# Keeping Softplus's table loaded, converting one weight group a tile, and letting the second MLP begin after one chunk

## The chip, the cores and the metric

The kernel runs on one core of one Trainium2 chip. The metric is the device time of one execution in microseconds (us), a median of several runs. PE is TensorE, DVE is VectorE, ACT is ScalarE, POOL is GpSimd; SP issues the DMAs.

## What is computed

Top-32 attention over 4 batches of 8 heads (576 rows, head size 64), then two MLPs on its 2304 x 512 output, the first with a softplus between its two matrices, the second with h - tanh(h). The weights arrive as float64.

```python
scores = scale * np.matmul(q, k.transpose(0, 1, 3, 2))
kth = np.partition(scores, -32, axis=-1)[..., -32:-31]
scores = np.where(scores >= kth, scores, -1e9)
attn = np.exp(scores - scores.max(-1, keepdims=True))
attn = attn / (attn.sum(-1, keepdims=True) + 1e-09)
x = np.matmul(attn, v)              # then heads side by side: 2304 x 512
h = x @ w_in;  x = (np.maximum(h, 0) + np.log1p(np.exp(-np.abs(h)))) @ w_out
h = x @ w2_in; out = (h - np.tanh(h)) @ w2_out      # 512 -> 2048 -> 512, both
```

## The kernel before

**Attention** goes in 144 tiles of 128 query rows (one head and one batch each; 16 of them gather the rows that are left over). A tile runs through a pipeline: `front` (L582) makes the 128 x 576 scores on PE and ACT copies them out (L585, tile `ssb`); `chain` finds the 32nd largest on DVE with four MAX8 (L594) and three MATCH_REPLACE8 (L597), so that four MAX8 are one tile in every count below; `exps` takes the exponential on ACT; `turn` splits it into two 16-bit halves (L624 on ACT, L625 and L626 on POOL) and a DMA transposes them (L628, issued by SP); `back` multiplies by v (L640 to L645).

`exps` has two forms. With the table set of the exponential loaded, it is two ACT instructions over 128 x 576 (L134, out `ssb` and then out `x`). With Softplus's set loaded it is one (L134, out `x`); `mask` then adds a multiplication on DVE (L618) and a scaling on ACT (L619). Which form a tile takes follows from the set that is loaded as the program is written down. `set_table` (L128) loads a set.

**Weights** come in 32 groups, 8 for each of the four matrices, converted from float64 to two 16-bit halves by `conv_step`: two DVE passes (L316, L334), three ACT passes (L306, L310, L335), POOL (L342, L346), eight small PE matmuls (L192) and a DVE reduction (L199). A pass is over 128 x 1024, or four times over 128 x 256 where a group is loaded in quarters into spare x buffers. Groups 0 to 15 are the first MLP's, 16 to 31 the second's. `WPS` = 2 groups are issued a tile for the first 16 and `WPS2` = 0.5 after that, from tile 8 on; groups after the sixteenth get a lower priority than the attention.

**The MLPs** go in ten chunks: two of 256 rows for each batch, and two of 128 rows for the rows left over (each after two batches). A chunk is 8 steps of the first MLP and 8 of the second; a step (`mlp_step`) is `gemm1` (24 matmuls, L708 to L710), `act1` (Softplus or Tanh at L134, L727 on DVE for the second MLP, L729 on ACT, L730 and L733 on POOL) and, some steps later, `gemm2` (24 matmuls of 256 columns at L751 to L753 in the first MLP, 12 of 512 columns at L759 to L761 in the second). `y_finish` turns the first MLP's result into the second's input. A chunk can begin when its last attention tile is through, at tiles 19, 39, 55, 75 and so on.

**The planner**: each tile hands out one step of 256 rows (or two of 128). `next_step` picks: the second MLP of a chunk that waits when all 32 groups are converted, at least `MINC` chunks have begun, and two chunks wait (`AHEAD`); else the first MLP of the next chunk that is ready; else, with the same conditions on groups and `MINC`, the second MLP of a waiting chunk; else nothing, and the tile's step is lost (only one is carried over). A scheduler then places the instructions on each engine by priority; the engines run them in that fixed order.

Of the kernel before, what the change touches and what calls it, by code (L numbers as in the profile page):

```python
# [18 lines left out]
EXP_SET = "exp_and_others"  # L19
# [16 lines left out]
KE = 'P'  # L36
NQH = 1
OWN = 3
MINC = 2
HPW = 100  # L40
HPW2 = 0
MKN = 0
# [31 lines left out]
def topk_attention_two_mlps(  # L74
# [29 lines left out]
    NG = NF // 2  # L104
# [17 lines left out]
    def set_table(name):  # L122
        if table[2] == name:
            return
        with ExitStack() as es_:
            for i in table[1] or [table[0]]:
                es_.enter_context(tc.issue_after(i.ins))
            table[0] = nc.scalar.preload_act_table_set(name)  # L128
        table[1], table[2] = [], name
# [673 lines left out]
    def run_gemm2(stp):  # L803
        ch = stp.ch
        if stp.g == 0:
            acc = new_acc(ch.T)
            if stp.m == 0:
                ch.acc1 = acc
            else:
                ch.acc2 = acc  # L810
        stp.acc = ch.acc1 if stp.m == 0 else ch.acc2
        gemm2(stp)
        if stp.g == NG - 1:
            if stp.m == 0:
                y_finish(ch)
            else:
                out_finish(ch)
# [4 lines left out]
    def mlp_step(ch, m, g):  # L822

        if m == 1 and g == 0:
            while any(s.ch is ch and s.m == 0 for s in pend):
                run_gemm2(pend.pop(0))
        stp = Step()
        stp.ch, stp.m, stp.g, stp.T = ch, m, g, ch.T
        if m == 0:
            if g == 0:  # L830
                set_table(SP_SET)
                key = f"l{ch.b // 2}" if ch.left else f"b{ch.b}"
                if key not in scales1:
                    scales1[key] = chunk_scales(ch.ix if ch.left else ix[ch.b], 0, 1.0, "a" + key)
                ch.sc1 = scales1[key]
                ch.ic1 = ch.sc1[2]
            stp.x = ch.x
            stp.sc = ch.sc1
        else:
            if g == 0:  # L840
                set_table(EXP_SET)
                if not hasattr(ch, "sc2"):
                    ch.sc2 = second_scales(ch.sy, ch.iy)
            stp.x = ch.y
            stp.sc = ch.sc2
        gemm1(stp)
        if g == NG - 1 and m == 1:
            xy_free.extend(stp.x.slots)
        with tc.high_priority(100):
            act1(stp)  # L850
        if g == NG - 1 and m == 0:
            set_table(EXP_SET)
        pend.append(stp)
        while len(pend) > (LAG if ch.T == 2 * P else LAG1):
            run_gemm2(pend.pop(0))
# [81 lines left out]

    wloaded, wconv = [], []
    WPS = 2
    WPS2 = .5  # L940
    wi, wcred = [0], [0.0]
    wq = [(i, g) for i in range(4) for g in range(NG)]

# [35 lines left out]
    def next_step(n):  # L979

        if phase[0] is None:
            can1 = c1[0] < len(order) and order[c1[0]][1] <= n
            can2 = wdone[0] == 4 * NG and c1[0] >= MINC
            if can2 and len(kept) >= AHEAD:
# [23 lines left out]
    def emit_steps(n, budget):  # L1008
        nonlocal_credit[0] += budget
        while nonlocal_credit[0] > 0:  # L1010
            st = next_step(n)
            if st is None:
                nonlocal_credit[0] = min(nonlocal_credit[0], 1.0)
                return
            mlp_step(*st)
            nonlocal_credit[0] -= st[0].T / 256.0
# [24 lines left out]
    for n in range(-1, NT + 2 + BL):  # L1041
# [36 lines left out]
        if n >= 0:  # L1078
# [3 lines left out]
            if n in v_norm_at and n > 0:  # L1082
                b = v_norm_at[n]
                v_norm(b)
                if b % 2:
                    nc.vector.tensor_tensor(sxl[b // 2], sx[b - 1], sx[b], op=ALU.min)
                    nc.vector.tensor_tensor(ixl[b // 2], ix[b - 1], ix[b], op=ALU.max)
                    for c in (b - 1, b):
                        nc.vector.tensor_mul(fl[c], sxl[b // 2], ix[c])
            wcred[0] += WPS if wi[0] < 16 else (WPS2 if n >= W2N else 0)  # L1090
            while wcred[0] >= 1:
# [12 lines left out]
    while (st := next_step(NT)) is not None:  # L1104
        mlp_step(*st)
# [32 lines left out]
```

## Time and profile before

| | us |
|---|---|
| median of 3 runs | 1326.21 (1322.19 to 1329.95) |
| the profiled execution | 1331.09 |
| its span, first to last instruction | 1329.4 |
| PE busy (81%) | 1071.8 |
| DVE busy (75%) | 992.9 |
| ACT busy (70%) | 935.0 |
| POOL busy (63%) | 833.9 |

How to read the profile: a busy time is the time in which an engine had an instruction running; matmuls are pipelined, so a busy PE isn't one at its peak. The line of slices cuts the span into 40 equal parts, a digit for the busy tenths of each. PEclk, or the granted clock, is the share of TensorE's full clock. A row of windows gives for a stretch of time the busy time of each engine with, in brackets, the number of its instructions.

### The profile page before, as it was taken

Reading aid. Unit: us, or ns where it says so; the run is one execution under the profiler, and the core shown is the slowest. Engines: PE = TensorE matmul, PEld = TensorE weight load, DVE = VectorE, ACT = ScalarE, POOL = GpSimd, SP = SyncE. Lnnn points to the kernel's source line nnn. Section 1 sums busy time; section 2 is a strip of 40 time slices with the busy share of each in tenths; the row PEclk is TensorE's granted clock in tenths of the full one; section 3 lists DMA queues with packets and bytes.
Section 4 is the critical chain, followed back from the end, with each engine's and each line's share of the span. In section 5 each row is a group of like instructions: output and inputs, shape, how many; then the busy total and the mean of one; then the engine's idle time right before and its main releaser. Section 6 shows DMA issues by size and latency. Waiting matters only on the chain.

```text
span 1329.4 us, 28005 instructions
## 1 busy us (share of the span) xinstructions
PE 1071.8 (81%) x9992; PEld 834.9 (63%) x9992; DVE 992.9 (75%) x2208; ACT 935.0 (70%) x1824; POOL 833.9 (63%) x1196
## 2 busy tenths in 40 slices
PE   3242436894358998999899999999999799999998
PEld 2241325673236866767677886686767677886975
DVE  5997988989889498986899699849978699620011
ACT  7967868787777688775877777668866777743332
POOL 3879776676766666664678566657855466543332
PEclk9999998895558899998899999999999899999999
DMA  9956787357647647553455344545654345200000
GB/s 283 302 141 192 211 224 174 82 122 159 149 116 172 137 97 156 132 97 91 92 126 140 72 92 86 96 90 100 139 85 94 72 92 95 41 14 9 9 9 17
DMA packets 322524, 153.17 MB, mean 115 GB/s; under 512 B 270160, under 2 KB 302416, under 8 KB 322384
## 3 DMA queue, kind: packets, MB, share of 16 engines
q1 hardware_dynamic: 322384, 151.39, 49.5%
q8 instruction: 78, 1.28, 0.4%
q14 instruction: 62, 0.51, 0.1%
HBM read 73.04 MB, written 15.37 MB: 67 GB/s over the span
## 4 chain that ended last, share of the span: by engine, by line
PE 37%; DMA 14%; DVE 13%; ACT 13%; POOL 12%; issue 8%; SPq 2%; POOLq 0%; ACTq 0%; DVEq 0%
PE h L710 5%; PE h L708 5%; PE h L709 5%; DMA pT<-hl 5%; DVE m L594 4%; DVE x L597 4%; POOL hl L625 3%; PE y L760 2%; PE y L759 2%; PE y L761 2%; PE y L751 2%; PE y L752 2%; PE y L753 2%; PE s L582 2%; POOL g L733 2%
## 5 line engine op out<-in xcount | busy, mean ns | idle before, releaser
L594 DVE MAX8 m<-x 128x8 f32<-128x576 f32 x432 | 318.1, 748 | 2.7
L625 POOL TENSOR_TENSOR hl<-x,hl 128x512 f16<-128x512 f32 x144 | 173.1, 1202 | 96.2 <-ACT hl L624 86.8
L730 POOL TENSOR_SCALAR r<-r,gs 128x512 f32<-128x512 f32 (+1 forms) x160 | 110.5, 691 | 177.0 <-ACT g L729 164.1
L597 DVE MATCH_REPLACE8 x<-m,x 128x576 f32<-128x576 f32 x288 | 213.1, 740 | 0.0
L733 POOL TENSOR_TENSOR g<-r,g 128x512 f16<-128x512 f32 (+1 forms) x160 | 173.2, 1084 | 9.1
L708 PE MATMUL h<-y,whi 128*128 128x256 f16 (+1 forms) x640 | 164.4, 266 | 9.7 <-ACT y L779 9.3
L708 PE MATMUL h<-x,whi 128*128 128x256 f16 (+1 forms) x640 | 165.6, 268 | 4.1 <-DMA x<-xs 3.6
L751 PE MATMUL y<-g,whi 128*128 128x256 f16 (+1 forms) x640 | 163.6, 266 | 5.3 <-ACT o L791 3.3
L752 PE MATMUL y<-g,whi 128*128 128x256 f16 (+1 forms) x640 | 164.4, 267 | 1.7 <-POOL g L733 1.7
L710 PE MATMUL h<-x,wlo 128*128 128x256 f16 (+1 forms) x640 | 165.6, 268 | 0.0
L709 PE MATMUL h<-x,whi 128*128 128x256 f16 (+1 forms) x640 | 165.5, 267 | 0.0
L753 PE MATMUL y<-g,wlo 128*128 128x256 f16 (+1 forms) x640 | 164.4, 267 | 0.0
L710 PE MATMUL h<-y,wlo 128*128 128x256 f16 (+1 forms) x640 | 164.1, 266 | 0.0
L709 PE MATMUL h<-y,whi 128*128 128x256 f16 (+1 forms) x640 | 164.1, 265 | 0.0
L727 DVE SCALAR_TENSOR_TENSOR r<-h,hin,r 128x512 f32<-128x512 f32 (+1 forms) x80 | 55.0, 689 | 142.3 <-ACT r L134 141.6
L134 ACT ACTIVATE r<-h,hin 128x512 f32<-128x512 f32 (+1 forms) x160 | 102.2, 640 | 82.6 <-PE h L710 71.2
L582 PE MATMUL s<-kT,qT 128*128 128x288 f16 x512 | 117.7, 324 | 40.4 <-ACT ssb L585 31.3
L729 ACT ACTIVATE g<-r,gs 128x512 f16<-128x512 f32 (+1 forms) x160 | 107.9, 676 | 56.8 <-PE y L752 22.7
L594 DVE MAX8 m<-ssb 128x8 f32<-128x576 f32 x144 | 107.9, 750 | 50.4 <-ACT ssb L585 50.0
L709 PEld LDWEIGHTS <-whi 128*128 128x128 f16 x1280 | 127.0, 99 | 23.0 <-issue 5.0
L708 PEld LDWEIGHTS <-whi 128*128 128x128 f16 x1280 | 127.6, 100 | 20.5 <-issue 0.3
L640 PE MATMUL px<-vhl,pT 128*128 128x65 f16 (+1 forms) x640 | 96.9, 208 | 52.9 <-DMA pT<-hl 51.8
(143 smaller groups left out, 3160.0 us busy)
## 6 DMA issues: line engine op xcount, KB each, us to landing
whi<-in_moe_w_in_dram SPq DMA_DIRECT2D x8, 1024.0 KB, 5.7
wlo<-in_moe_w_in_dram SPq DMA_DIRECT2D x6, 1024.0 KB, 7.4
wlo<-in_moe_w_out_dram SPq DMA_DIRECT2D x6, 1024.0 KB, 5.1
vd<-vhl SPq DMA_DIRECT2D x16, 330.0 KB, 3.3
vhl<-vd SPq DMA_DIRECT2D x16, 330.0 KB, 3.3
kd<-kT SPq DMA_DIRECT2D x32, 160.0 KB, 2.2
whi<-in_moe_w_out_dram SPq DMA_DIRECT2D x5, 1024.0 KB, 5.3
kT<-kd SPq DMA_DIRECT2D x32, 160.0 KB, 2.6
```

Of the source, the lines that this page charges most:

```text
L582: nc.tensor.matmul(ps[:, hf, 0:HS], lhs, rhs[:, hf * HS : (hf + 1) * HS], start=(i == 0), stop=(i == len(prods) - 1))
L594: return lambda: nc.vector.max(m[:, 8 * i : 8 * i + 8], src)
L597: return lambda: nc.vector.match_replace(x, m[:, 8 * i : 8 * i + 8], src, NEG)
L625: nc.gpsimd.tensor_sub(hl[:, S + SL : 2 * S], st.p[:, 0 : NB * P], hl[:, 0 : NB * P])
L708: nc.tensor.matmul(o, hi[:, f], xhi, start=(d == 0), stop=False)
L709: nc.tensor.matmul(o, hi[:, f], xlo, start=False, stop=False)
L710: nc.tensor.matmul(o, lo[:, f], xhi, start=False, stop=(d == ND - 1))
L730: nc.gpsimd.tensor_scalar(r, r, gs, 1.0, op0=ALU.mult, op1=ALU.mult)
L733: nc.gpsimd.tensor_sub(glo, r, ghi)
L751: nc.tensor.matmul(o, hi[:, dd], gh, start=first, stop=False)
L752: nc.tensor.matmul(o, hi[:, dd], gl, start=False, stop=False)
L753: nc.tensor.matmul(o, lo[:, dd], gh, start=False, stop=fin)
```

## The change

`MINC` goes from 2 to 1: the second MLP may begin when one chunk has begun the first. `WPS2` goes from 0.5 to 1: groups 16 to 31 are issued one a tile. The load of the exponential's table set at the end of each chunk's first MLP goes; the set is still loaded where a second MLP begins.

```diff
-MINC = 2
+MINC = 1
...
         with tc.high_priority(100):
             act1(stp)
-        if g == NG - 1 and m == 0:
-            set_table(EXP_SET)
         pend.append(stp)
...
     WPS = 2
-    WPS2 = .5
+    WPS2 = 1
```

The first place is DVE at attention tiles 32 and 33 (`ssb` in, first MAX8 of the tile). Before, passes over the last weight matrix stand there (`whi3`, `wlo3`).

```order
L316 SCALAR_TENSOR_TENSOR whi3_98<-whi3_98 128x256
L597 MATCH_REPLACE x_600_3125<-m_599_3124,x_600_3125 128x576
L597 MATCH_REPLACE x_615_3217<-m_614_3216,ssb_608_3160 128x576
L316 SCALAR_TENSOR_TENSOR wlo3_99<-wlo3_99 128x256
L334 SCALAR_TENSOR_TENSOR whi3_98<-whi3_98 128x256
L316 SCALAR_TENSOR_TENSOR wlo3_99<-wlo3_99 128x256
L594 MAX m_599_3124<-x_600_3125 128x8
L594 MAX m_614_3216<-x_615_3217 128x8
L316 SCALAR_TENSOR_TENSOR whi3_98<-whi3_98 128x256
```

After the change, with steps of the second MLP (`r`, L727):

```order
L594 MAX m_684_3785<-ssb_677_3722 128x8
L594 MAX m_651_3592<-x_652_3593 128x8
L597 MATCH_REPLACE x_669_3687<-m_668_3686,x_669_3687 128x576
L597 MATCH_REPLACE x_685_3786<-m_684_3785,ssb_677_3722 128x576
L597 MATCH_REPLACE x_652_3593<-m_651_3592,x_652_3593 128x576
L727 SCALAR_TENSOR_TENSOR r_614_3388<-h_613_3363,hin_610_3356,r_614_3388 128x512
L594 MAX m_668_3686<-x_669_3687 128x8
L594 MAX m_684_3785<-x_685_3786 128x8
L727 SCALAR_TENSOR_TENSOR r_627_3473<-h_626_3448,hin_610_3356,r_627_3473 128x512
```

What moved: the weight passes stand earlier, all 32 groups before tile 28 instead of tile 40, and the second MLP's steps stand where there was none.

The second place is ACT at the end of the attention, from the last softmax exponential on (out `x`, in `ssb`). Before, steps of the left-over chunk's first MLP (128x256) follow:

```order
L134 ACTIVATE x_2657_16088<-ssb_2643_15976,nb_2693_16405,tiny_84 128x576
L664 ACTIVATE x32_2662_16115<-px_2660_16099,r2_2663_16116 128x64
L134 ACTIVATE r_2665_16145<-h_2664_16120,hin_2644_15979 128x256
L729 ACTIVATE g_2666_16146<-r_2665_16145,gs_2645_15980 128x256
L619 ACTIVATE x_2657_16088<-x_2657_16088 128x576
```

After the change, steps of the second MLP of batch 3's first chunk (128x512):

```order
L134 ACTIVATE x_2693_16558<-ssb_2686_16464,nb_2723_16760,tiny_84 128x576
L624 CAST hl_2724_16764<-x_2693_16558 128x576
L656 ACTIVATE r2_2710_16678<-px_2707_16661,tiny_84 128x1
L664 ACTIVATE x32_2709_16677<-px_2707_16661,r2_2710_16678 128x64
L134 ACTIVATE r_2701_16613<-h_2700_16588,hin_2641_16091 128x512
L729 ACTIVATE g_2702_16614<-r_2701_16613,gs_2642_16092 128x512
```

What moved: behind that exponential stand 38 steps before (24 of 256 rows, 14 of 128), and 31 after (23 and 8).

The third place is ACT where batch 1's second chunk ends its first MLP and the left-over chunk begins its own (`r`, 128x512 and then 128x256). Before, two table loads stand between, with one softmax in the exponential's form:

```order
L134 ACTIVATE r_1638_9344<-h_1637_9319,hin_1222_6742 128x512
L128 ACT_TABLE_LOAD
L134 ACTIVATE ssb_1600_9085<-ssb_1600_9085,m_1606_9151 128x576
L729 ACTIVATE g_1639_9345<-r_1638_9344,gs_1223_6743 128x512
L134 ACTIVATE x_1607_9152<-ssb_1600_9085,nb_1641_9381,tiny_84 128x576
L128 ACT_TABLE_LOAD
```

After the change:

```order
L134 ACTIVATE r_1594_9159<-h_1593_9134,hin_1119_6279 128x512
L619 ACTIVATE x_1578_9072<-x_1578_9072 128x576
L664 ACTIVATE x32_1564_8982<-px_1602_9210,r2_1603_9225 128x64
L624 CAST hl_1620_9353<-x_1578_9072 128x576
L672 CAST xs_1563_8981<-x32_1564_8982 128x128
L729 ACTIVATE g_1595_9160<-r_1594_9159,gs_1120_6280 128x512
```

What moved: the two loads are gone, and the softmax between takes Softplus's form. Over the program the loads go from 20 to 16 and the tiles in Softplus's form from 53 to 59. One weight group more is loaded and converted in quarters (56 instructions at L316, from 53).

## Rows read from the trace of the kernel before

**Rows 1.** The page: 40 slices of PE, DVE and granted clock.

```profile
PE   3242436894358998999899999999999799999998
...
DVE  5997988989889498986899699849978699620011
...
PEclk9999998895558899998899999999999899999999
```

**Rows 2.** Windows by stage: us, engines' busy us (instructions), clock, DMA.

```profile
core 0: us, PE busy (x) PEld busy (x) DVE busy (x) ACT busy (x) POOL busy (x), PEclk, DMA share, GB/s
0.00:151.60 151.60, 53.84 (x358) 42.64 (x358) 128.93 (x292) 114.67 (x186) 106.50 (x118) 1.00 0.77 225
151.60:301.30 149.70, 94.44 (x850) 77.46 (x850) 131.23 (x298) 117.41 (x227) 110.01 (x135) 0.95 0.65 158
301.30:391.60 90.30, 37.66 (x293) 25.62 (x294) 79.11 (x198) 67.58 (x150) 62.06 (x104) 0.50 0.62 145
391.60:461.20 69.60, 59.96 (x563) 51.34 (x563) 49.77 (x141) 52.65 (x119) 44.95 (x72) 0.85 0.71 154
461.20:1150.70 689.50, 652.61 (x6284) 502.56 (x6282) 575.59 (x1228) 514.58 (x1026) 439.24 (x672) 0.97 0.48 100
1150.70:1329.40 178.70, 173.25 (x1650) 135.23 (x1648) 28.29 (x57) 68.12 (x120) 71.09 (x100) 0.99 0.07 16
```

**Rows 3.** Timeline of PE in the tail: start us, us, instruction.

```profile
1239.77 0.27 PE L709 MATMUL h<-x,whi 128*128 128x256 f16 x1
1239.88 0.27 PE L710 MATMUL h<-x,wlo 128*128 128x256 f16 x1
1239.99 0.27 PE L708 MATMUL h<-x,whi 128*128 128x256 f16 x1
...
1242.72 0.27 PE L752 MATMUL y<-g,whi 128*128 128x256 f16 x1
```

**Rows 4.** Windows of L199 alone, a group being two instructions of it.

```profile
36.50:123.70 87.20, 3.73 (x22) 1.00 0.69 197
151.60:301.30 149.70, 3.14 (x18) 0.95 0.65 158
301.30:391.60 90.30, 2.08 (x12) 0.50 0.62 145
```

**Rows 5.** Windows of L594 alone, a tile being four of it.

```profile
36.50:123.70 87.20, 19.31 (x27) 1.00 0.69 197
301.30:391.60 90.30, 36.24 (x51) 0.50 0.62 145
391.60:461.20 69.60, 20.75 (x29) 0.85 0.71 154
461.20:1150.70 689.50, 277.85 (x385) 0.97 0.48 100
464.50:511.00 46.50, 23.40 (x33) 1.00 0.54 108
```

**Rows 6.** Windows of L708 alone: eight are one step.

```profile
301.30:391.60 90.30, 0.00 (x0) 0.00 (x0) 0.50 0.62 145
464.50:511.00 46.50, 17.18 (x63) 6.24 (x64) 1.00 0.54 108
...
1150.70:1329.40 178.70, 71.54 (x304) 29.90 (x304) 0.99 0.07 16
```

**Rows 7.** The whole span of L316, then of L334, alone.

```profile
0.00:1329.40 1329.40, 58.02 (x53) 0.93 0.50 115
...
0.00:1329.40 1329.40, 54.77 (x53) 0.93 0.50 115
```

**Rows 8.** Groups of instructions: busy us, mean ns, idle before and its releasers.

```profile
L618 DVE SCALAR_TENSOR_TENSOR x<-ssb,m,x 128x576 f32<-128x576 f32 x53 | 49.0, 925 | 28.6 <-ACT x L134 28.6
L619 ACT ACTIVATE x<-x 128x576 f32<-128x576 f32 x53 | 36.1, 681 | 7.6 <-DVE x L618 7.2
L134 ACT ACTIVATE ssb<-ssb,m 128x576 f32<-128x576 f32 x91 | 69.5, 773 | 16.1 <-DVE m L594 15.7
L128 ACT ACT_TABLE_LOAD x20 | 25.7, 1283 | 0.4
```

**Rows 9.** Waits: PE, then SP's queue; us in total, times, longest.

```profile
PE h L708 <- ACT y L779: 9.3, 2, 5.2
...
SPq L292 <- POOL wlo L346: 14.8, 5, 6.6
```

**Rows 10.** Windows: the slice of the page with the second MLP's direct start.

```profile
1030.29:1063.50 33.22, 26.44 (x252) 22.04 (x250) 22.57 (x51) 23.45 (x43) 14.40 (x25) 0.85 0.35 72
```

## The prediction

> **What bounds the kernel now.** I read the slices of the page first [rows 1]. PE is poorly used for about 430 us, then nearly always busy; DVE is busy until the attention ends near 1150 us; behind that PE works alone. The granted clock of PE falls to half (1.2 of 2.4 GHz) in the slices from 299 to 399 us, where PE has nothing but attention to do.
>
> The windows give this stage by stage [rows 2]; I cut them at attention tiles, by the MAX8 on DVE. Up to 301 us (tiles 0 to 27) and again to 391.6 us (tiles 28 to 39) DVE has the most to do: 131.2 of 149.7 us, 79.1 of 90.3 us. From 461.2 to 1150.7 us PE is busy 652.6 of 689.5 us and DVE 575.6 us. In the tail PE is busy 173.3 of 178.7 us and DVE 28.3 us. So the kernel has a stage that DVE sets, with an idle PE, then one in which both are nearly full, and a tail that PE sets. Work that PE can do in the first stage instead of the tail is a gain; work that the first stage gets on DVE is a cost.
>
> **The change, part by part.**
>
> A, the tail. By the planner's rules, tiles 26 to 38 hand out no step before: the next chunk isn't ready, and the second MLP waits for the weights and for a second chunk. In the changed program the weights are issued by tile 23, the first chunk's second MLP takes tiles 26 to 33, and the tiles without a step are 34 to 38, 54, 70 to 74 and 130: twelve instead of thirteen. A tile after such a gap hands out two steps, and there are three more of these. So only four steps of 256 rows leave the tail, not eight: by the order on ACT, 24 + 14/2 = 31 steps of 256 rows stand behind the last softmax exponential before, 23 + 8/2 = 27 after. A step is 48 matmuls' worth of 256 columns, and these start (1242.72 - 1239.77)/27 = 0.109 us apart in the tail, the last row shown being the 27th after the first [rows 3]: 48 x 0.109 = 5.2 us. Four of them are 20.9 us. DVE and ACT are far from full there, so nothing else is late: **-21 us**.
>
> B, tiles 11 to 27. The order on DVE has six more groups' reductions there than before, 15 for 9 (the second row of [rows 4] has the 9). What a group costs where groups are on the path comes from two stretches. Between 36.5 and 123.7 us, with two groups issued a tile, 11 groups and 27/4 = 6.75 tiles took 87.2 us [rows 4, 5]. A tile without a group takes 5.64 us: 46.5 us for 33/4 tiles, with 63/8 steps of the second MLP beside them [rows 5, 6]. So a group took (87.2 - 38.1)/11 = 4.5 us. Between 301.3 and 391.6 us it was (90.3 - 12.75 x 5.64)/6 = 3.1 us. By DVE's two big passes alone it is (58.0 + 54.8)/32 = 3.5 us [rows 7]. The upper end is 6 x 4.5 = 27 us. The lower end is 3 us, if the 18.5 us that DVE is idle in the second stage [rows 2] all take conversion: 6 x 3.5 - 18.5. I take 4.0 a group, since the rate of one group a tile lies between the two stretches and DVE's idle time there is mostly waiting inside the chains: **+24 us**.
>
> C, tiles 28 to 39. The six groups leave: -6 x 3.1 = -18 us. Eight steps of the second MLP come; [rows 5, 6] show that tiles with such steps take 5.64 us, the figure that I used for a tile without any, so beside a free PE they cost nothing more. What they do need is the first chunk's result: its first MLP ends later now, and behind tile 28's scores stand 32/8 steps of gemm1 and 38/8 of gemm2 in one piece on PE, some (4 + 4.75) x 2.6 = 23 us. Before, such a piece stood at tile 27 and DVE filled it with conversions. Ends: -27 us (4.5 a group) and +8 us (PE's 38 us of attention at half clock, or some 19 at full, with 42 us of steps, 23 us of that piece and 7 us of the gap below make 91 to 110 us, some of it at either clock, for 90.3). I take **-15 us**, near the rows of the very stretch.
>
> D, tiles 40 to 143. They hold four steps less than before (7 tiles without a step, 3 with two). If PE sets the pace that is worth -21 us; if DVE does, a tile without a step saves 689.5/96.25 - 5.64 = 1.5 us [rows 2, 5], 7 of them 11 us, and the tiles with two steps give some of it back. Against it, one more chunk has its second MLP right behind its own first (batch 0's second chunk), where PE waits for y_finish: 9.3 us in two such places before [rows 9], and PE is idle 6.8 us and has a clock of 0.85 in the slice around one [rows 10]. Ends -21 and +7; I take **-7 us**, as both engines are nearly full in this stage.
>
> E, the table. Four loads go, 4 x 1.28 = 5.1 us of ACT; six more softmaxes take the other form: 0.93 us more on DVE each, and on ACT 0.68 instead of 0.77 us [rows 8]. ACT has time throughout, so the loads are worth nothing by themselves; DVE gets 5.6 us, in stages where it is 80 to 90% busy. Ends 0 and +6: **+3 us**.
>
> SP. The weight loads are issued earlier, and one more group goes in quarters. A load waits for its buffer on SP's queue, and the attention's transposes stand behind it there; before, five such waits came to 14.8 us, the longest 6.6 us [rows 9]. They lie in the stretches of B, and the bounds of B hold them.
>
> Sum: -21 + 24 - 15 - 7 + 3 = **-16 us**. The profiled execution took 1331.1 us for its span of 1329.4, and the median of the runs is 1326.2, 0.4% below it. I take the difference from the median: **1310 us**. What this kernel's measurement can tell from no change is about 0.5%, 6.6 us.
>
> **Rivals.**
>
> 1. Slower: each gap makes the first MLP behind it start anew. Between 391.6 and 461.2 us, behind the one long gap of before, 29/4 = 7.25 tiles took 9.6 us each, at a clock of 0.85, against 7.16 us in the steady stage [rows 2, 5]: 17.7 us more. The changed program keeps that restart at tile 39 and adds gaps ahead of tiles 55, 75 and 131. If two of the three cost 18 us, the sum is -16 + 36 = +20 us: 1346 us. It decides from about one and a third such restarts on. For it: PE was busy 60 of 69.6 us there though DVE was only 49.8. Against it: the new gaps are one or five tiles long, not thirteen, and gemm2 of the steps before still runs in them. The Trainium skill bears on this ("TensorE: Matmul & The Clock Gate", Part 1): the array's clock is at half by default and activity lets it up, so idle stretches are paid by the work behind them. The trace agrees: 0.50 granted in the gap, 0.85 in the stretch after it [rows 2]; that speaks against a change that makes three gaps of one.
>
> 2. No difference: the conversions cost their upper end (B +27, C -12) and D gives nothing, since DVE sets the tiles that PE leaves. -21 + 27 - 12 + 0 + 5 = -1 us: 1325 us. For it: DVE's 83% in the steady stage and its waits inside each tile's chain. Against it: PE's 95%.
>
> 3. More: PE sets the steady stage throughout, D is -21 us, and the sum -30: 1296 us. For it: PE's 95% busy, and PE's weight loads are busy 502.6 of 689.5 us (73%) there against 135.2 of 178.7 us (76%) in the tail, which PE surely sets [rows 2]. The Trainium skill ("Perfetto Trace Analysis", Identifying the Most-Contended Engine) holds the share of weight loads for a better measure of PE than matmul time; by it the two stages are nearly alike, which is this rival's case. Against it: the 9.6 us tiles and the gaps show waiting that isn't PE's work.
>
> 4. It doesn't do what it says: the later groups have low priority, and if their conversion still ended near tile 39 in time, the second MLP couldn't fill the gap: about 1326 us. The order stands against it, with all 32 groups converted before tile 28.
>
> **How the numbers follow.** The forecast has a chance of 0.42 (0.36 of it below 1319.6, 0.06 within 0.5%); rival 1 0.17, all slower; rival 2 0.20 (0.04 faster, 0.12 within, 0.04 slower); rival 3 0.17, faster; rival 4 0.04, within. That makes 0.57 faster, 0.22 within 0.5%, 0.21 slower. The likeliest case is the forecast, 1310 us, and its own range 1300 to 1322. The ends of the terms all at once would reach from 1272 (-21 + 3 - 27 - 21 + 0, less what B and C can't both have, since a group cheap to take in is cheap to give up: some 12 us back) to 1353; leaving out a tenth on each side, and with rivals 2 and 3 inside, the range is 1286 to 1338.
>
> **What would show it.** A: L708 has about 304 - 56 = 248 instructions behind the last tile's first MAX8 [rows 6] (seven steps of any size), and that stretch takes near 158 us. B and C: tile 28 begins near 325 us (from 301), tile 40 near 400 (from 392), the clock in between is well over 0.5, and L708 is no longer absent there. D: tiles 40 to 143 take near 752 us (759 before, 391.6 to 1150.7). E: 16 loads, 59 at L618. Rival 1 would show as tiles of over 9 us with a clock under 0.9 behind the gaps at 54 and 70 to 74, rival 2 as tile 40 past 407 us and D unchanged. Wrong would be the whole account if the tail shortened by 21 us and B and C still came to over +40: then a group costs far more than 4.5 us once 16 stand so close.

## The result, and the profile after

The changed kernel took 1342.56 us (median of 20 runs, 1329.24 to 1349.36) against 1325.62 us (20 runs, 1318.11 to 1329.95): a ratio of 1.0116, interval 1.0093 to 1.014. It is slower by 1.2%, where 1310 us was forecast. The profiled execution was one of its quickest, 1334.75 us for a span of 1333.0; a second one (run `a_again` below), 1345.38 us for 1343.6, lies nearer the median, so both stand in the account below.

The page's slices of PE, DVE and granted clock, to set beside [rows 1]:

```profile
PE   3242445287896879998969899998999899999998
...
DVE  5998999975599989877899888758888788840011
...
PEclk9999999997798989998989999889999899999999
```

A slice is 33.3 us now. PE's hole between 299 and 399 us is filled and its clock there is 0.7 to 0.9, where it was 0.5; in its place DVE, full before, reads 7, 5 and 5 from 267 to 367 us. The windows by stage, cut at the first MAX8 of attention tiles 20, 24, 27, 28, 40, 48 and 143, show the same in numbers (columns as in [rows 2]):

```profile
core 0: us, PE busy (x) PEld busy (x) DVE busy (x) ACT busy (x) POOL busy (x), PEclk, DMA share, GB/s
0.00:234.90 234.90, 94.70 (x658) 75.10 (x659) 212.73 (x497) 188.46 (x332) 180.59 (x198) 1.00 0.82 226
234.90:269.40 34.50, 9.64 (x54) 5.94 (x53) 32.58 (x75) 23.39 (x51) 22.79 (x29) 1.00 0.43 119
269.40:303.20 33.80, 25.34 (x244) 21.55 (x243) 26.25 (x52) 23.87 (x51) 28.40 (x43) 0.97 0.31 76
303.20:351.50 48.30, 42.05 (x317) 30.50 (x316) 17.63 (x64) 24.23 (x59) 22.74 (x38) 0.77 0.36 81
351.50:424.80 73.30, 60.08 (x541) 41.44 (x539) 68.61 (x144) 58.99 (x126) 49.13 (x83) 0.93 0.63 136
424.80:486.50 61.70, 55.23 (x558) 47.77 (x559) 54.00 (x124) 50.88 (x109) 44.05 (x64) 0.98 0.74 171
486.50:1170.40 683.90, 640.05 (x6201) 492.88 (x6201) 579.90 (x1221) 497.89 (x1005) 428.93 (x665) 0.95 0.49 97
1170.40:1333.00 162.60, 158.23 (x1429) 120.54 (x1426) 25.48 (x52) 61.67 (x104) 63.33 (x85) 1.00 0.07 16
```

One row stands out. From the first MAX8 of tile 27 to that of tile 28 pass 48.3 us, and DVE works in 17.6 of them. Before, tiles 24 to 27 together took 37.0 us (264.3 to 301.3). In us, by stretches:

| | before | after | after, second profile | difference | forecast |
|---|---|---|---|---|---|
| to tile 28 | 301.3 | 351.5 | 355.7 | +50.2, +54.4 | +24 (B) |
| tiles 28 to 39 | 90.3 | 73.3 | 72.8 | -17.0, -17.5 | -15 (C) |
| tiles 40 to 143 | 759.1 | 745.6 | 752.4 | -13.5, -6.7 | -7 (D), +3 (E) |
| tail | 178.7 | 162.6 | 162.7 | -16.1, -16.0 | -21 (A) |
| span | 1329.4 | 1333.0 | 1343.6 | +3.6, +14.2 | -16 |

Behind tile 28 each stretch came near its term in number. The loss lies in B. By the rows above and [rows 2], DVE works 289.2 us up to tile 28, for 260.2 before, and stands idle 62.3 us, for 41.1: of the 50.2 us, 29.0 are more work and 21.2 are more idle time. What the engines wait for in the long tile (engine, instruction, what ended the wait: us in total, times, longest):

```profile
DVE r L657 <- ACT r L656: 11.3, 3, 7.6
...
ACT r L134 <- PE h L710: 6.3, 1, 6.3
DVE x L597 <- POOL hl L626: 6.0, 1, 6.0
```

On DVE's timeline of that tile (start, us, instruction, in brackets the idle time ahead of it and what ended it) the last weight passes and the attention's own small steps alternate with gaps of 3 to 8 us:

```profile
305.36 0.43 DVE L334 SCALAR_TENSOR_TENSOR wst<-wst 128x256 int32<-128x256 int32 x1
309.08 0.16 DVE L205 TENSOR_SCALAR n<-pn 128x1 int32<-128x1 int32 x1 [3.29 <-PE pn L169]
...
315.93 0.09 DVE L597 MATCH_VALUE_LOAD x<-m,ssb 128x8 f32 x1 [5.95 <-POOL hl L626]
...
335.08 0.76 DVE L594 MAX8 m<-x 128x8 f32<-128x576 f32 x1
343.45 0.16 DVE L657 RECIPROCAL r<-r 64x2 f32<-64x2 f32 x1 [7.61 <-ACT r L656]
351.55 0.76 DVE L594 MAX8 m<-ssb 128x8 f32<-128x576 f32 x1 [7.94 <-ACT ssb L585]
```

ACT's timeline says what those two last waits stood behind:

```profile
341.16 0.69 ACT L134 ACTIVATE r<-h,hin 128x512 f32<-128x512 f32 x1 [6.35 <-PE h L710]
341.87 1.28 ACT L128 ACT_TABLE_LOAD   x1
343.16 0.26 ACT L656 ACTIVATE r<-px,tiny 64x2 f32<-64x2 f32 x1
...
350.88 0.64 ACT L585 COPY ssb<-s 128x576 f32<-128x576 f32 x1
```

ACT waits 6.35 us for a step of the first MLP on PE; the attention's L656 stands behind that in ACT's order, and DVE's reciprocal behind L656. L656 itself could not have run much sooner: PE starts the last of its tile's matmuls (L645) at 341.12 us, in turn with that step. The next MAX8 waits for the copy at L585. PE had made its scores by 304.7 us (L582 at 302.61, 2.10 us, is the last before the copy), so it waits for its place in ACT's order alone, behind work that came late: ACT is busy 10.17 of the last 10.20 us (the last row below). The Trainium skill ("DVE: scalar operands, raw-bit mode, write accounting and state across instructions", Flops that outlive an instruction) calls DVE's queue one in-order queue; the trace fits that, since nothing else on DVE ran in those 15.5 us of waiting, though it doesn't show that anything else was ready.

PE was the late one at the start of this. Four windows of the long tile: from 331.0 us on PE is busy throughout, at a granted clock of 0.72 and 0.78, so for part of the time at the lower of its two levels (1.2 GHz; the last section has what it did there), and in the last of them DVE has 0.16 us of work:

```profile
303.20:318.50 15.30, 9.78 (x76) 7.48 (x75) 5.46 (x17) 5.57 (x16) 9.20 (x16) 0.72 0.32 75
318.50:331.00 12.50, 11.77 (x121) 9.65 (x121) 7.33 (x38) 6.06 (x16) 6.09 (x12) 0.86 0.47 88
331.00:341.30 10.30, 10.30 (x51) 5.18 (x52) 4.67 (x10) 2.43 (x6) 4.19 (x5) 0.72 0.42 98
341.30:351.50 10.20, 10.20 (x74) 8.19 (x73) 0.16 (x1) 10.17 (x23) 3.25 (x6) 0.78 0.22 67
```

### The profile page after: what moved, and what is told of

The parts are those of the page before. It is cut to its first block, busy times and chain, and to the rows that moved or that the text cites. A ratio compares the mean times of both kernels' runs of the same rounds, so it can differ in the third digit from the quotient of the medians.

```text
span 1333.0 us, 28027 instructions
## 1 busy us (share of the span) xinstructions
PE 1085.3 (81%) x9992; PEld 835.7 (63%) x9992; DVE 1017.2 (76%) x2220; ACT 929.4 (70%) x1829; POOL 840.0 (63%) x1201
## 4 chain that ended last, share of the span: by engine, by line
PE 47%; DVE 12%; DMA 12%; ACT 10%; POOL 10%; issue 7%; SPq 2%; POOLq 0%; ACTq 0%; DVEq 0%
PE h L709 7%; PE h L710 7%; PE h L708 7%; DMA pT<-hl 4%; DVE m L594 4%; PE y L759 4%; PE y L760 4%; PE y L761 4%; DVE x L597 3%; PE s L582 3%; PE y L752 2%; PE y L753 2%; PE y L751 2%; POOL wlo L346 2%; POOL hl L625 2%
## 5 line engine op out<-in xcount | busy, mean ns | idle before, releaser
L594 DVE MAX8 m<-x 128x8 f32<-128x576 f32 x432 | 319.4, 750 | 4.0
L708 PE MATMUL h<-y,whi 128*128 128x256 f16 (+1 forms) x640 | 165.6, 267 | 7.9 <-ACT y L779 5.6
L708 PE MATMUL h<-x,whi 128*128 128x256 f16 (+1 forms) x640 | 167.0, 268 | 0.3 <-DMA x<-xs 0.3
L751 PE MATMUL y<-g,whi 128*128 128x256 f16 (+1 forms) x640 | 163.7, 268 | 3.0 <-ACT g L729 2.3
L594 DVE MAX8 m<-ssb 128x8 f32<-128x576 f32 x144 | 108.3, 752 | 63.7 <-ACT ssb L585 63.1
L727 DVE SCALAR_TENSOR_TENSOR r<-h,hin,r 128x512 f32<-128x512 f32 (+1 forms) x80 | 55.2, 690 | 129.2 <-ACT r L134 127.8
L582 PE MATMUL s<-kT,qT 128*128 128x288 f16 x512 | 117.0, 321 | 38.2 <-ACT ssb L585 34.6
L708 PEld LDWEIGHTS <-whi 128*128 128x128 f16 x1280 | 127.4, 100 | 21.3
L134 ACT ACTIVATE x<-ssb,nb,tiny 128x576 f32<-128x576 f32 x144 | 123.8, 864 | 23.6 <-DVE m L594 13.6
```

Source lines behind the costliest of these rows:

```text
L134: table[1].append(nc.scalar.activation(out, in_, func, **kw))
L582: nc.tensor.matmul(ps[:, hf, 0:HS], lhs, rhs[:, hf * HS : (hf + 1) * HS], start=(i == 0), stop=(i == len(prods) - 1))
L594: return lambda: nc.vector.max(m[:, 8 * i : 8 * i + 8], src)
L708: nc.tensor.matmul(o, hi[:, f], xhi, start=(d == 0), stop=False)
L751: nc.tensor.matmul(o, hi[:, dd], gh, start=first, stop=False)
```

## Experiments

Times are medians beside runs of the kernel before on the same chip. The columns "tile 40" and "143" are the first MAX8 of these tiles in the profiled execution, "DVE idle" the time to tile 40 less DVE's busy time in it, "soft" the softmaxes in Softplus's form (instructions at L618), all in us but the last. The interval of a ratio is 3 to 5 us to either side, so a difference of less than some 5 us between two rows is not clear of noise. T1 to T4 are the theories 1 to 4 of the expectations below.

| kernel | median, ratio (95%) | tile 28 | tile 40 | DVE idle | 143 | span | soft |
|---|---|---|---|---|---|---|---|
| before | 1325.62 | 301.3 | 391.6 | 52.3 | 1150.7 | 1329.4 | 53 |
| changed | 1342.56, 1.0116 | 351.5 | 424.8 | 67.0 | 1170.4 | 1333.0 | 59 |
| a_again | 1342.56, 1.0128 (1.0093 to 1.0163) | 355.7 | 428.5 | 65.6 | 1180.9 | 1343.6 | 59 |
| e_wps2_only | 1344.32, 1.0141 (1.0104 to 1.0179) | 354.8 | 422.1 | 72.7 | 1165.9 | 1344.5 | 53 |
| e_wps2_2 | 1351.36, 1.0186 (1.0155 to 1.0216) | 361.0 | 434.8 | 77.0 | 1183.6 | 1346.3 | 59 |
| e_no_table | 1336.53, 1.008 (1.005 to 1.0111) | 354.2 | 430.3 | 72.0 | 1175.5 | 1334.7 | 50 |
| g_before | 1333.65, 1.0058 (1.0031 to 1.0085) | 292.0 | 395.0 | 54.8 | 1158.6 | 1337.7 | 53 |
| g_wps2 | 1328.11, 1.0004 (0.998 to 1.0027) | 301.3 | 404.7 | 53.7 | 1147.3 | 1325.9 | 53 |
| e_w2n24 | 1348.45, 1.0148 (1.0114 to 1.0183) | 277.5 | 367.1 | 48.6 | 1169.0 | 1348.1 | 53 |
| t_w667 | 1321.98, 0.9958 (0.9936 to 0.9981) | 317.4 | 411.8 | 59.4 | 1160.9 | 1320.1 | 50 |
| t_w75 | 1322.89, 0.9976 (0.9953 to 0.9998) | 322.3 | 421.3 | 64.4 | 1168.2 | 1327.4 | 50 |
| t_w6 | 1319.13, 0.9949 (0.9927 to 0.9971) | 318.2 | 403.7 | 54.8 | 1158.2 | 1317.4 | 52 |
| a_w667 | 1343.19, 1.0132 (1.0101 to 1.0162) | 306.8 | 426.5 | 65.4 | 1179.0 | 1341.7 | 64 |
| e_table_only | 1340.06, 1.0105 (1.0077 to 1.0132) | 289.8 | 392.3 | 45.7 | 1158.2 | 1343.7 | 74 |
| x_first | 1336.37, 1.0092 (1.006 to 1.0124) | 287.5 | 390.3 | 45.8 | 1155.9 | 1334.7 | 67 |
| x_late | 1312.46, 0.9897 (0.9863 to 0.9931) | 297.6 | 385.2 | 50.3 | 1121.0 | 1307.3 | 60 |
| x_loads | 1342.82, 1.0131 (1.0097 to 1.0166) | 294.1 | 386.5 | 48.2 | 1157.8 | 1336.3 | 74 |
| x_w667_late | 1329.88, 1.0037 (1.0011 to 1.0064) | 314.1 | 407.6 | 57.2 | 1161.1 | 1323.8 | 58 |
| a_late | 1343.69, 1.012 (1.0086 to 1.0154) | 354.2 | 430.8 | 70.9 | 1181.5 | 1344.6 | 58 |
| x_w6_late | 1324.26, 0.9982 (0.9955 to 1.001) | 311.8 | 398.0 | 54.8 | 1162.0 | 1325.0 | 60 |

### Which edit makes the loss: the rate of the later groups

The changed kernel once more, and the kernel before with `WPS2` alone:

> The changed kernel as it is, once more. Its profiled execution took 1334.8 us, 8 us less than its median, so this one is to show where the other executions lose more. All theories: 1342 us, give or take 5. Theory 1 (the last weight groups meet the end of the first chunk's first MLP): tile 27 (first MAX8 of 27 to that of 28) takes 45 us or more again. Theory 3 (direct starts and gaps): the further time lies behind tile 40, at the gaps.

```diff
-    WPS2 = .5
+    WPS2 = 1
```

> The kernel before with WPS2 = 1 alone. Theory 1: the long tile 27 is there without any step of the second MLP behind it (over 40 us), and since tiles 28 to 39 have no conversions left they give back some 20 us, so 1335 to 1350 us. Theory 3 (the direct start of the second MLP makes the stall): no long tile, the conversions only move, 1322 to 1332 us.

The long tile comes again: 47.5 us at tile 27 in the changed kernel, and with `WPS2` alone 58.4 us at tile 26 (291.4 to 349.8), four steps of the first MLP in it. `WPS2` alone makes the whole loss, and the same hole on DVE, though no step of the second MLP stands near; so T3 falls, and T1's 1335 to 1350 us came. Windows of the kernel with that edit alone:

```profile
264.00:303.00 39.00, 31.32 (x274) 25.72 (x274) 31.18 (x70) 24.88 (x54) 29.29 (x43) 0.96 0.33 73
303.00:349.80 46.80, 37.94 (x310) 28.48 (x311) 14.96 (x60) 23.66 (x55) 19.98 (x32) 0.85 0.31 72
```

Its tiles 28 to 39 take 67.3 us, 23.0 less than before, and the changed kernel with the load put back, the same plan plus eight steps of the second MLP there, 76.1: 8.8 us for eight steps. In the medians `MINC` so gives back 7.8 us of what `WPS2` costs (1336.53 against 1344.32; the intervals overlap a little).

### Groups, or groups beside the first MLP

The kernel before with no step of any MLP ahead of tile 28, and that kernel with `WPS2 = 1`:

```diff
-            can1 = c1[0] < len(order) and order[c1[0]][1] <= n
+            can1 = c1[0] < len(order) and order[c1[0]][1] <= n and n >= 25
```

> The kernel before with no MLP step before tile 28 (next_step gets the condition n >= 25): the first chunk's first MLP runs in tiles 28 to 35, and everything else is as before. Both theories: 1320 to 1345 us; it is the partner of g_wps2 below.

> The same with WPS2 = 1: the later groups are converted by tile 29, with no MLP step among them. Theory 1 (six groups cost 20 to 30 us by themselves; the rest of the 54 us is the first chunk's MLP that they push back into one piece, in which DVE waits): tile 28 begins 15 to 30 us later than in g_before, and tiles 28 to 40 take 15 to 25 us less, so that the end is within 10 us of g_before. Theory 4 (a group costs 9 us wherever it stands, once they come one a tile): tile 28 begins 45 us or more later, and the end is 20 us or more later.

Windows to tile 28, g_before and then g_wps2:

```profile
0.00:292.00 292.00, 111.44 (x848) 86.04 (x849) 252.31 (x592) 220.05 (x399) 201.08 (x238) 0.90 0.73 199
0.00:301.30 301.30, 114.12 (x809) 89.00 (x810) 269.22 (x624) 233.69 (x431) 221.12 (x264) 1.00 0.73 200
```

By the reductions at L199, four groups more stand ahead of tile 28 in g_wps2 (31 for 27; 32 for 26 with the first MLP there). Tile 28 begins 9.3 us later, 2.3 us a group, with 16.9 us more work on DVE and 7.6 us less idle time: by themselves the groups take DVE's time and part of its gaps. With the first chunk's first MLP beside them (e_wps2_only against the kernel before) tile 28 begins 53.5 us later. At tile 40, where all groups are converted in all four kernels, the delay is 9.7 us without that MLP and 30.5 with it, 20.4 of the 30.5 being DVE's idle time (at 54.8 and 53.7 us it doesn't grow in the g pair). In the medians the same edit gains 5.5 us without it and costs 18.7 with it. So T4 falls, and the interplay of the two is worth 20 us and more.

Of g_wps2 T1 had only the end right, within 10 us of g_before: it wanted tile 28 15 to 30 us later, and tiles 28 to 39 shorter by 15 to 25 us, but they took as long (103.4 for 103.0 us); tiles 40 to 47 gave the time back, 58.5 for 72.0 us.

Two more tries to move the groups away from the first chunk, the changed kernel with two groups a tile, and the kernel before with the later groups held back to tile 24 and then issued one a tile:

```diff
-    WPS2 = 1
+    WPS2 = 2
```

> The changed kernel with WPS2 = 2: all groups are converted before the first MLP's steps are in full flow (by the order on PE before tile 23), so that no conversion stands between the last steps of the first chunk's first MLP. Theory 1: tile 27 is under 30 us, tile 40 begins 15 to 30 us earlier than in the changed kernel (424.8 us), 1315 to 1328 us. Theory 2 (the table) and theory 3 (direct starts and gaps), which this leaves alone: 1337 to 1350 us.

```diff
-    W2N = 8
+    W2N = 24
...
-    WPS2 = .5
+    WPS2 = 1
```

> The kernel before with WPS2 = 1 and W2N = 24: groups 16 to 31 are issued one a tile in tiles 24 to 39, in the gap behind the first chunk's first MLP, none beside it. Theory 1: tile 24 begins some 25 us earlier than before (264.3 us) without a long tile behind it, tile 40 within 12 us of before (391.6 us), 1315 to 1335 us. Theory 4 (9 us a group): tile 40 past 430 us, 1360 us or more.

Both ends were missed, and both show a hole on DVE elsewhere. With two groups a tile, tiles 20 to 23 take 62.2 us (30.9 before), DVE working in 43.7 of them; no matmul stands at L708 in the first 45.8, so this hole is not the first MLP's, and what makes it was not found. With the later groups in tiles 24 to 39, tile 40 comes 24.5 us earlier than before and the second chunk's first MLP then makes the piece, 40 matmuls at L708 and 46 at L751 in tile 46, which takes 38.5 us, 15.8 of them DVE's work. The last conversion instruction starts at 422.3 us there (POOL, L346), 13 us ahead of that tile: the piece needs no group beside it; that the groups ahead of it push the MLP's steps together is argued, not shown. A window of the latter kernel:

```profile
367.10:476.90 109.80, 69.66 (x626) 56.99 (x626) 71.54 (x184) 73.28 (x164) 68.92 (x113) 0.73 0.52 124
```

That is tiles 40 to 47, 73.0 us before.

### A lower rate, without the table edit

The changed kernel with the load put back (`e_no_table`), and that with lower rates:

```diff
+        if g == NG - 1 and m == 0:
+            set_table(EXP_SET)
...
-    WPS2 = 1
+    WPS2 = .667
```

> The changed kernel with the load of the exponential's set back at the end of each first MLP: the edit of the table undone alone (softmaxes in Softplus's form 50, from 59). Theory 2 (the table costs: nine softmaxes at 0.93 us on DVE and what waits for them): 1330 us or less. Theories 1 and 3: 1337 to 1347 us, within 6 us of the changed kernel.

> The changed kernel with the table loads back (as e_no_table, 1336.5 us) and WPS2 = 0.667: two groups in three tiles, the second MLP of the first chunk begins at tile 31 instead of 26, and the first chunk's first MLP begins by the order on PE at tile 20 instead of 24, in smaller pieces. The steps left behind the attention are the changed kernel's. Theory 1: tile 40 begins 10 to 25 us earlier than in e_no_table (430.3 us), 1312 to 1327 us. Theory 4: the same number of groups by tile 40, 1334 to 1342 us.

> The changed kernel with the table load put back and WPS2 = 0.75. In its order 24 matmuls of gemm1 at L708, 46 of gemm2 at L751 and 28 of conversion at L192 still stand in one piece behind tile 27's scores, nearly as with WPS2 = 1, though a quarter fewer groups are issued a tile. T1: the long tile 27 is there again (over 30 us) and the time is 1330 to 1340 us, near that with WPS2 = 1 (1336.5) and not halfway to the 1322 of WPS2 = 0.667. T4 (the rate of groups sets the cost): the gain is in proportion, 1326 to 1331, and no tile takes over 25 us.

> The changed kernel with the table load put back and WPS2 = 0.6. The piece behind tile 27's scores is 16 matmuls at L708, 16 at L192, 30 at L751; the second MLP begins near tile 38. T1: no tile of 20 to 28 over 25 us, tile 40 near 412 us, and 1318 to 1325 us in all. T4: in proportion to the groups a tile, 1318 to 1322. Neither: over 1330.

`e_no_table` came between the theories, half a us outside T1's range. The lower the rate, the less DVE is idle before tile 40 (72.0, 64.4, 59.4, 54.8 us), and tile 40 moves from 430.3 to 403.7. The three lower rates beat the kernel before by 0.2 to 0.5%. T1 has 0.667 right, tile 40 18.5 us earlier and 1312 to 1327 us. With 0.75 the long tile is there (tile 26, 32.0 us), but the time is 1322.89, not the 1330 to 1340 that T1 wanted, nor T4's 1326 to 1331. With 0.6 the time is in both ranges, but tile 26 takes 29.6 us, where T1 wanted none over 25. So the loss is not set by one piece: in these four kernels it falls with DVE's idle time. That doesn't hold across the table (`a_w667` has 65.4 us of it and 1343.19). Windows of tile 26 with 0.667 and of tile 26 with 0.75, the longest ahead of tile 28 in each:

```profile
287.20:313.20 26.00, 16.77 (x144) 13.30 (x144) 16.73 (x45) 15.62 (x32) 15.94 (x25) 0.76 0.25 63
```

```profile
284.40:316.40 32.00, 31.88 (x322) 27.92 (x321) 17.80 (x50) 22.92 (x50) 23.77 (x37) 0.94 0.31 58
```

### The table edit

The whole change with the lower rate, and the table edit alone on the kernel before:

> The changed kernel whole, table edit and MINC included, with WPS2 = 0.667 in place of 1 as the one number that differs. T1: the piece at tile 27 is gone, so 10 to 25 us under the changed kernel: 1318 to 1332 us, and tile 28 before 325 us. T2: the table edit costs its 3 to 8 us against the 1322 of the same rate with the load put back: 1325 to 1330. If the loss were in MINC or the table edit and not in the place of the first MLP: 1338 us or more.

```diff
-        if g == NG - 1 and m == 0:
-            set_table(EXP_SET)
```

> The kernel before with the table edit alone (the exponential's set is not loaded at the end of a first MLP; WPS2 0.5, MINC 2). 74 softmaxes take Softplus's form for 53; the steps of the MLPs stay where they were. T2 (the edit costs by itself, as the difference of 6 us between the changed kernel and the one with the load put back suggests): 0.3 to 1 us a tile of the other form, 21 more tiles, so 1330 to 1345 us, spread over tiles 28 to 143. T1 (only where the first MLP stands matters): within 3 us of 1326, and tile 28 within 3 us of the kernel before.

Both went against T1. Alone the edit costs 14.5 us, inside T2's 1330 to 1345; at the rate of 0.667 it costs 21.2, well past T2's 3 to 8, where it costs 6.0 in the changed kernel. Of the 14.3 us that the edit alone adds to the span of the profiled execution, 6.8 lie behind the attention: two steps more stand there (320 instructions at L708 for 304), though the steps were to stay where they were. At 0.667 tile 28 comes early (306.8), but the conversions end later, and some five steps of the second MLP, 42 instructions at L708, fall into one tile, the 37th, of 30.7 us. The window from tile 36 to tile 40:

```profile
377.40:426.50 49.10, 45.61 (x384) 32.10 (x384) 35.32 (x82) 33.07 (x75) 32.12 (x55) 0.88 0.60 124
```

The edit was then split by place. The first chunk alone, and every chunk but the first, on the kernel before; the second of these also on the other rates:

```diff
-        if g == NG - 1 and m == 0:
+        if g == NG - 1 and m == 0 and c1[0] > 1:
             set_table(EXP_SET)
```

> The kernel before with the table edit for the first chunk alone: the exponential's set is not loaded where chunk 00 ends its first MLP, and is loaded as before behind every later one. 67 softmaxes take Softplus's form for 53 (the edit for all chunks: 74, and 14.5 us slower), nearly all in tiles 26 to 39, where no MLP step runs. F (each tile in Softplus's form costs the same, 14.5/21 = 0.7 us): 14 of them, +10 us, so 1333 to 1339 us. P (the cost is in the later chunks, where PE and DVE are both nearly full; the profile of the whole edit shows tile 40 only 0.7 us later than before): within 4 us of 1326.

```diff
-        if g == NG - 1 and m == 0:
+        if g == NG - 1 and m == 0 and c1[0] == 1:
             set_table(EXP_SET)
```

> The other half: the kernel before with the table edit for every chunk but the first. 60 softmaxes in Softplus's form for 53. F: 7 x 0.7 = +5 us, so 1328 to 1333 us. P: nearly the whole 14.5 us, 1336 to 1342 us, with tile 40 within 3 us of before.

> The changed kernel with WPS2 = 0.667 and the table edit for every chunk but the first: 58 softmaxes in Softplus's form, against 50 with the load put back everywhere (1322 us) and 64 with the whole edit (1343 us). If the first chunk's part makes the 15 us that the whole edit loses before tile 40 at this rate (the conversions pushed to later tiles, 48 matmuls of gemm1 in one piece behind tile 37): 1325 to 1331 us, tile 40 near 412 us. F: 1322 + 8 x 0.7 = 1328. If the later chunks make it: 1338 or more.

> The changed kernel with the first chunk's load of the exponential's set put back, the later ones left out as in the change: 58 softmaxes in Softplus's form, 59 in the changed kernel (1342.6), 50 with all loads back (1336.5). If the first chunk's part of the edit is what costs here as it does alone (+10 us) and at 0.667 (+13): 1328 to 1334 us. If the later part costs as it does at 0.667 (+8): within 4 us of 1342.6. If it gains as it does on the kernel before (-13.6): under 1328 us.

> The two edits that gained, together: WPS2 = 0.6 and MINC = 1 (1319.1, 6.5 us under the kernel before) and the table edit for every chunk but the first (1312.5 alone, 13.6 under). 60 softmaxes in Softplus's form. If the gains were prices that add: 1306 us. If each only comes with the order that the scheduler happens to make: anywhere from 1312 to 1330.

And the loads themselves, two in the place of each that the edit leaves out:

```diff
         if g == NG - 1 and m == 0:
             set_table(EXP_SET)
+            set_table(SP_SET)
```

> The kernel with the table edit alone, and in the place of each load that the edit leaves out two, the exponential's set and then Softplus's again: the same forms of softmax, 20 more loads on ACT, 20 x 1.28 = 26 us of it. If ACT's time is worth nothing, as step E has it, this stays at the 1340 of the edit alone, within 4 us. If loads count in full: 1360 us or more; in between a price a load can be read.

```profile
L128 ACT ACT_TABLE_LOAD x34 | 43.6, 1283 | 0.4
```

Twenty loads more than with the edit alone, 25.6 us of ACT, cost 2.8 us (1342.82 against 1340.06, intervals overlapping). Loads are next to free here, as step E had it. The Trainium skill ("ScalarE: Activation LUTs", What ACT_TABLE_LOAD costs) gives 2.66 us for a switch, its drain included, by estimate 53 us for twenty. The 1283 ns of the load agree; the drain doesn't show, since ACT's next instruction starts 1.29 or 1.30 us after the load does, at 33 of the 34 loads; and the end of the program moved by 0.14 us a load.

The parts don't add. The first chunk's part costs 10.3 us alone, the later part gains 13.6, both together lose 14.5. The later part costs 7.9 us at 0.667 and 7.2 in the changed kernel (a_late against e_no_table), where the first part costs nothing (-1.1). With 0.6 the later part costs 5.1 where a sum of gains would have been 1306. F has the first chunk's part right (1333 to 1339) and the later part at 0.667 (1328), but misses `x_late` by 15 us and more; P misses both halves. So neither holds. Two kernels show it best. Between the first MAX8 of tile 48 and that of tile 143, x_late and e_table_only load tables nine times and make 45 softmaxes in Softplus's form, both, and start 823 and 818 matmuls at L708; one takes 670.8 us and the other 691.1. The kernel with the edit alone, then that with the later part:

```profile
467.10:1158.20 691.10, 652.73 (x6171) 497.71 (x6169) 585.39 (x1221) 501.48 (x1013) 435.22 (x667) 0.96 0.49 99
```

```profile
450.20:1121.00 670.80, 641.20 (x6183) 495.76 (x6181) 580.08 (x1223) 502.77 (x1015) 437.13 (x668) 0.97 0.50 102
```

PE is busy 11.5 us longer for as many matmuls and idle 8.8 us longer. Up to 8.7 of the 11.5 us are the pairs of unlike matmuls that the last section shows (102 of them, 42.6 us, for 89, 33.9 us). They don't settle it: the kernel with the extra loads has 67 of them, 26.1 us, and takes 690.9 us from tile 48 to tile 143. In DVE's order only 1966 of the 2215 and 2229 instructions stand in one common order (by operation and tile), though the edit only concerns the first chunk. What of that order is worth the 20 us was not found; no experiment here could change the work and keep the order.

## Why the prediction was wrong

**A** was the right mechanism, somewhat too large: -16 for -21. L708 has 255 instructions in the tail (the second row below), 49 fewer than before [rows 6], where 56 fewer were forecast, and PE's busy time there fell from 173.3 to 158.2 us, three steps of 5.2 us and not four (with the load put back the tail is 159.2 us, 19.5 less than before):

```profile
303.20:351.50 48.30, 9.13 (x32) 3.13 (x32) 0.77 0.36 81
1170.40:1333.00 162.60, 62.98 (x255) 25.02 (x255) 1.00 0.07 16
```

The other row, L708 in the long tile, has the 32/8 steps that the next point is about.

**B failed**, and with it the forecast: +50 to +54 for +24. The step priced a group from two stretches in which no MLP runs, 3.1 and 4.5 us [rows 4, 5], and added six of them. Without an MLP four groups cost 2.3 us each, below both, since DVE's idle time took part of them. What was missing is the first chunk's first MLP in the same tiles. It begins on PE at tile 23 instead of tiles 19 and 20, with the last groups' conversion, and its four last steps lie between tile 27 and tile 28. The bound of 27 us held groups alone; the interplay, some 20 us of idle DVE, had no term. The sentence that names the piece stands in C: it put 23 us of PE work behind tile 28's scores, beside a stretch that PE and DVE share, and said that DVE had filled such a piece with conversions before. It should have asked whether DVE still could, with ACT's and DVE's orders waiting for that very piece. The 23 us were also priced at the tail's 0.109 us a matmul: in the long tile PE was busy 42.1 us, at a clock of 0.77 and in part with pairs of matmuls that took 0.36 us and more (the last section). The tile took 48 us, and DVE worked in 17.6 of them.

**C** came out at -17 for -15, from two wrong halves, so by luck. Read without the table edit, the groups that leave are worth -23.0 us (3.8 each, not 3.1), and the eight steps that come cost 8.8 us, not nothing, together -14.2: DVE has 5.9 us at L727 and 1.4 at L780 before tile 40 that it hadn't before.

**D** and **E**: tiles 40 to 143 took 745.6 and 752.4 us; 752 was forecast. The number came by luck. `WPS2` alone takes no step out of these tiles and still brings them to 743.8 us, 15.3 less than before, 11.6 of it in tiles 40 to 47; in the changed kernel tiles 48 to 143 took 683.9 and 690.4 us for 686.1. So the gain is not shown to be that of the four steps. In the changed kernel the table edit is worth 6.0 us in the medians, the upper end of 0 to +6, all of it in the later chunks. The loads fell to 16 and L618 rose to 59, as read from the order (groups with busy us, mean ns, idle time ahead):

```profile
L128 ACT ACT_TABLE_LOAD x16 | 20.5, 1283 | 0.3
...
L618 DVE SCALAR_TENSOR_TENSOR x<-ssb,m,x 128x576 f32<-128x576 f32 x59 | 58.6, 993 | 14.9 <-ACT x L134 14.7
```

The working of E, a difference of DVE's busy time per softmax, is no price that carries over: the edit, or a part of it, moved other programs from -13.6 to +21.2 us.

**The rivals.** Rival 1 gave 1346, near the time, by another way: behind the gap tiles 40 to 47 took 61.7 us, less than the 73.0 of before, at a clock of 0.98, and tiles 54 to 61 and 75 to 82 took 7.5 and 6.7 us each on the mean, where it wanted over 9. Nor does the gap alone make a restart: with `WPS2` alone it stays empty, at a clock of 0.53, and tiles 40 to 47 take 61.3 us at 0.96. What made them slow before was not tested.

Rival 2 wanted tile 40 past 407, which came, but from conversions at 27 us and an unchanged D, which didn't. Rival 3's D of -21 didn't come (-13.5 and -6.7). Rival 4 fell: 64 matmuls at L708 stand in tiles 28 to 39. The condition named as the end of the account, B and C over +40 with a shorter tail, was nearly met (+33 to +37), but the reading given for it, that a group costs far more than 4.5 us, is the one that the pair of g_before and g_wps2 excludes.

The table shows the trade that the change makes. Earlier groups and second steps ahead of tile 40 save time behind it: 937.8 us from tile 40 to the end before, 908.2 and 915.1 in the changed kernel, 908.3 with 0.667, 913.7 with 0.6. Not all of it is the second steps' doing: `WPS2` alone, which puts none there, has 922.4. What decides is the cost ahead of tile 40: 33 to 37 us at one group a tile, 20 at 0.667, 12 at 0.6. The best kernels here are the one with the rate of 0.6 and the load put back, 1319.13 us, and the kernel before with the later part of the table edit, 1312.46 us.

## What to carry to other kernels

Price moved work in the stretch where it arrives, beside what runs there: two things that each fit into an idle engine can hold each other up when every engine runs a fixed order, and the loss then shows as idle time on the engine that sets the pace. Look in the order for steps of another stage that fall in one piece between two tiles, and ask which engine's next instruction stands behind them. And where a scheduler rewrites the order at each edit, a price from one program doesn't add to that from another: here single edits of no great work moved the time by 1% either way.

## What the runs showed that was not expected

A busy PE is no sign of the high clock. In the long tile PE was busy 42.05 of 48.30 us at a granted clock of 0.77. Its windows from 331.0 us on show the clock fall while PE is busy without a break:

```profile
331.00:335.40 4.40, 4.40 (x27) 2.46 (x27) 4.23 (x10) 2.29 (x5) 2.83 (x4) 1.00 0.85 182
335.60:341.30 5.70, 5.70 (x24) 2.55 (x25) 0.24 (x1) 0.14 (x1) 1.16 (x2) 0.50 0.09 32
```

What PE does there is slow at either clock. Matmuls of gemm1 (256 columns) stand in turn with those of an attention tile (65 columns). Rows of PE's timeline: two of gemm2 first, then such a pair with a tile of 128 rows, one with the left-over tile, whose weights are 128*64, and one with the left-over tile later:

```profile
305.14 0.42 PE L752 MATMUL y<-g,whi 128*128 128x256 f16 x1
305.36 0.42 PE L753 MATMUL y<-g,wlo 128*128 128x256 f16 x1
...
324.64 0.27 PE L710 MATMUL h<-x,wlo 128*128 128x256 f16 x1
324.75 0.19 PE L641 MATMUL px<-vhl,pT 128*128 128x65 f16 x1
324.78 0.27 PE L708 MATMUL h<-x,whi 128*128 128x256 f16 x1
...
332.61 0.28 PE L710 MATMUL h<-x,wlo 128*128 128x256 f16 x1
332.82 0.22 PE L641 MATMUL px<-vhl,pT 128*64 128x65 f16 x1
332.97 0.28 PE L708 MATMUL h<-x,whi 128*128 128x256 f16 x1
...
339.11 0.39 PE L710 MATMUL h<-x,wlo 128*128 128x256 f16 x1
339.44 0.26 PE L642 MATMUL px<-vhl,pT 128*64 128x65 f16 x1
339.63 0.39 PE L708 MATMUL h<-x,whi 128*128 128x256 f16 x1
```

In the tail a matmul of 256 columns starts every 0.109 us [rows 3]. The two of gemm2 start 0.22 us apart, 18 in a row from 304.50 us on 0.213 on the mean; the Trainium skill ("TensorE: Matmul & The Clock Gate", Wait — 56ns, not 53.3ns?) gives columns over 1.2 GHz for that, 0.213 us for 256, and the trace agrees. A pair takes 0.14 us with the tile of 128 rows, and 0.36 us with the left-over tile, at a granted clock of 1.00 (0.52 at 0.50). The weight loads show a difference, of the 65-column matmuls at 324.75 and 332.82:

```profile
324.64 0.10 PEld L641 LDWEIGHTS <-pT 128*128 128x128 f16 x1
...
332.82 0.11 PEld L641 LDWEIGHTS <-pT 128*64 128x64 f16 x1
```

The first starts 0.11 us ahead of its matmul, the second together with it. Why the 128*64 weights are not loaded ahead is not shown. In the long tile 22 pairs of the left-over tile take 9.5 us, and the chain of work that ended last runs through them, from 330.94 to 341.16 us; at 0.14 us each they would take 3.1, an estimate from the rows above. The kernel before has no such pair ahead of tile 40 and 90 behind it. They don't make the long tile alone: with the rate of 0.6, 22 of them stand in tile 26, which takes 29.6 us.
